# New float64 conversion steps and new planner costs in an attention, experts and dense kernel

## The chip, the cores and the metric

The kernel runs on one core of one Trainium2 chip. The metric is the device time of one execution in microseconds (us). A core has five engines with a queue each, served in order: TensorE (PE, matmuls; PEld is its weight loads), VectorE (DVE), ScalarE (ACT), GpSimd (POOL) and SyncE (SP, which here only issues transfers). Queues of transfers hang on SP, ACT and POOL.

## The reference, cut to what matters

```python
# x (8, 8, 512, 64), state (8, 8, 32, 64)
xread = softmax(x @ state.T / 8) @ state           # per batch and head
sread = softmax(state @ x.T / 8) @ x
x = concat(xread, sread) -> (4352 tokens, 512)
# experts: 8 of them, each token goes to the one with the greatest logit
idx = argmax(normalise(x) @ normalise(expert_emb).T / tau)
out[idx == e] = gate * relu(x @ w1[e]) @ w2[e]     # w1 (8, 512, 1024), w2 (8, 1024, 512)
# dense network; w_in (512, 2048) and w_out (2048, 512) are float64
h = x @ w_in
return (h * clip(h + 3, 0, 6) / 6 @ w_out).astype(float32)
```

The two dense weights arrive as float64, so the kernel gets their bits as pairs of 32-bit words.

## The kernel before, in words

**Stages.** Attention goes batch by batch (8 batches) and writes every token's row to a buffer in DRAM. Routing gives each token a place in one of up to 41 slots of 128 tokens of one expert. Five leading slots belong to the expert with the most tokens and share its weights (QUAD and FIFTH); then come pairs of slots and single slots, each unit with weights of its own. Their results, sorted, go to DRAM, and the dense network takes them in 17 blocks of 256 tokens. All large products are done in three matmuls of float32r parts (high x high, high x low, low x high), so weights and activations are split into a high part (a cast) and a low part (the difference).

**Expert weights.** A load brings 512 KB into one of two raw buffers (`load_w`, lines 1231 and 1234, issued by SP). Each half is cast (line 1245, ACT or DVE) and its low part taken (line 1248, DVE or POOL). Matmuls of the first product are line 1409 (pairs and QUAD) and 1450 (singles), of the second line 1512.

**Dense network.** For a block, `Y` (lines 1575 and 1579) loads 256 rows; `F1` (line 1618) does 12 matmuls of 256 columns for each of 16 pieces m, then Relu (ACT, 1622), a product (DVE, 1625), a cast (ACT, 1629) and a low part (DVE, 1632); `F2` (line 1653) does 6 matmuls of 512 columns. F1 and F2 of piece m need the converted pieces ("i", m) and ("o", m).

**Conversion of the dense weights** (class `Conv`, function `convert`): 32 pieces of 128x512 float64. Eight are converted beside attention, six beside the leading slots, in two raw buffers of their own (`acr`). The other 18 follow when the leading slots are done (`opened`); their raw data lie in the second buffers of the tiles `yh` and `yw`, of which a block needs one pair, so there are two pieces at a time, and block 1 can't be loaded before the last piece has gone. A piece passes these steps:

- `load`: ACT issues the transfer (line 259 or 262).
- `cs` (DVE): line 271 shifts the top 16 bits of each number down to its exponent and writes it over the lowest 16 bits; line 272 masks the top mantissa bits into a new tile.
- `ct` (ACT): line 276 turns the exponents into those of bfloat16, in place; line 277 turns the mantissa bits into a float32 from 1 to 2.
- `cd` (DVE): line 281 puts the sign into the bfloat16, in place; line 282 adds the next 16 mantissa bits.
- `cp` (line 286, POOL, or DVE for late pieces): mantissa times signed power of two. Here the raw buffer is given back.
- `ch` (line 293, ACT): the high part. `cl` (line 296, POOL or DVE): the low part. Here the mantissa tile is given back.

So the exponents are 16-bit numbers 8 bytes apart, and mantissas lie side by side.

**Order.** The program runs a list scheduler (`Sched`, lines 39 to 126) when it is built. Every operation has a cost on one or more engines, a due time, operands and buffers of rings. The scheduler keeps a clock for each engine, takes the operation with the least start time plus a weight times its due time, lets it run on the cheaper engine where there are two, and emits it; that is the order of the queues. Due times come from a nominal order of TensorE's work (lines 1197 on) and of attention's batches (`OFF`), which the change leaves alone. For transfers of SP and ACT it also keeps a clock of the shared issue path:

```python
if e != "P":
    self.hw = b + 0.45 * (1 + o.cost[e] // 0.12)
```

Of the kernel before, what the change touches and what calls it, by code (L numbers as in the profile page):

```python
# [20 lines left out]
class Ring:  # L21
    """The buffers of a tag: the times from which those that nothing holds are free."""
# [5 lines left out]
class Hold:  # L28
    """A buffer of a ring, from the operation that takes it to the last of those that read it."""
# [9 lines left out]
class Sched:  # L39
    """Puts operations in the order of the engines' queues: by an estimate of the engines' times, an engine that  # L40
    is free takes the most urgent of the operations whose operands and buffers are there."""
# [9 lines left out]
    def op(self, fn, cost, prio, deps=(), take=(), give=(), dma=0.0, after=None):  # L51
        """After deps have ended, and behind after in the same queue."""
# [79 lines left out]
def kernel(  # L132
# [48 lines left out]
    # what is kept until the leading slots are done  # L181
# [40 lines left out]
    # ring buffers  # L222
# [12 lines left out]
    # the attention's end, the leading slots' end, and the end of the slots that may be left out  # L235
# [65 lines left out]
    def convert(n, prio, pool, ma, gate=None, start=0.0):  # L301
        """Takes over a piece: into the buffers of pool, from gate on."""
# [29 lines left out]
    # columns of the tokens: those of the last batches come last, BA before them  # L332
# [18 lines left out]
    # the state twice, for its transpose on both halves of the partitions  # L351
# [11 lines left out]
    # output row of every token slot of the internal order  # L363
# [3 lines left out]
    # as two numbers that bfloat16 holds  # L367
# [29 lines left out]
    # normalised expert embeddings over tau, transposed  # L397
# [15 lines left out]
    # state transposed, two heads block diagonal, its products with the embeddings, and its parts  # L413
# [49 lines left out]
    # ---- what is done with a batch  # L463
# [8 lines left out]
    # the first batches in larger pieces, with the heads outside  # L472
# [37 lines left out]
    # those of the reads of the tokens in parts, of the rows r0 to r1 of every partition  # L510
# [19 lines left out]
    # the scores with their signs turned, and their least ones: less the greatest scores  # L530
# [132 lines left out]
    def o_lg(b, r):  # L663
        """The logits of rows ahead of these."""
# [41 lines left out]
    # ---- the operations of the attention  # L706
# [44 lines left out]
    # the times of a batch's operations in the order of their urgency, and the engines of those that two can do  # L751
# [13 lines left out]
    def batch(b, t, last):  # L765
# [5 lines left out]
        def do(name, f, cost, *a, args=(), late=0.0, **k):  # L771
            """An operation of this batch; by the engine in BY if two can do it."""
# [33 lines left out]
        for v in range(2):  # L806
            e2.append(do("e2", o_e2, {"A": 0.664}, [mx[v]], [be2] if v == 0 else (), [hsc], args=(v,), late=v,
                         after=e2[-1] if e2 else None))
        r2 = do("r2", o_r2, {"D": 0.28}, e2)
        sd = do("sd", o_sd, {"P": 3.06}, g_ready[b], [bsd])  # L810
        for (r0, r1), scs in zip(chunks, scs_):
# [8 lines left out]
            nm = do("nm", o_nm, {"P": 0.1 + 0.00172 * n, "D": cd(n)}, [rc], args=rr)  # L820
# [6 lines left out]
        a2c = do("a2c", o_a2c, {"A": 0.904, "D": 1.131}, [a2], [ba2], [ha2])  # L827
# [4 lines left out]
        V["sxo", b] = do("sx", o_sx, {"D": 0.81}, [sr, r2], [sx_h[q]] if b % 4 == 0 else (), [hsr])  # L832
        late, w, a = 0, [], None
        lga_[b] = []
        for r in range(R):
# [5 lines left out]
            w.append(do(f"x{r}c", o_xrc, {"A": 0.491, "D": 0.615}, [a], (), [hp], args=(r,), late=r))  # L841
# [1027 lines left out]
```

## Time and profile before

| | us |
|---|---|
| median of 3 runs (least, greatest) | 1454.6 (1453.09, 1455.71) |
| span of the profiled execution | 1453.4 |
| PE busy in it | 1354.7 (93%), 8976 matmuls |
| DVE busy | 917.8 (63%) |
| ACT busy | 645.3 (44%) |
| POOL busy | 543.1 (37%) |

No time of the profiled execution as a whole is recorded beside its span; the median of the runs is 1.2 us above the span. The page cuts the span into 40 slices of 36.3 us; a digit is an engine's busy share in tenths:

```profile
PE   7896697877799999999999999999999999999997
DVE  6988888899976555645454544665666675433332
```

Busy time of an engine includes the time for which an instruction, once started, waits inside. A matmul counts as busy for as long as it takes, at whatever clock. Idle time of an engine that isn't the one that sets the pace costs nothing.

### The profile page before, as it was taken

What the parts mean: (1) busy time and instruction counts of PE and PEld (TensorE: products, weight loads), DVE (VectorE), ACT (ScalarE), POOL (GpSimd) and SP (SyncE); (2) the same over time, 40 slices, a digit from 0 to 9 for tenths busy, and PEclk for the clock granted to TensorE, in tenths of its full rate; (3) what the DMA queues carried; (4) which work ended last, traced back from release to release, by engine and by line L of the source; (5) the groups of instructions that cost most, each with busy time, mean ns of one, the idle gap of its engine ahead of it and who ended that gap; (6) DMA issues with size and microseconds to landing.
All of it is one profiled execution on the core that took longest, in us unless ns stands there. A gap on an engine that the chain in (4) does not pass through costs nothing. (4 is left out here: it accounts for less than half of the span.)

```text
span 1453.4 us, 25243 instructions
## 1 busy us (share of the span) xinstructions
PE 1354.7 (93%) x8976; PEld 1199.0 (82%) x8976; DVE 917.8 (63%) x2008; ACT 645.3 (44%) x1347; POOL 543.1 (37%) x558
## 2 busy tenths in 40 slices
PE   7896697877799999999999999999999999999997
PEld 6675686766688898989989898999998999899996
DVE  6988888899976555645454544665666675433332
ACT  4785435555643343434444343555544444333332
POOL 5554448566555232524142322244344322200000
PEclk8996689899899999999999999999999999999999
DMA  6643435555564333423243333555455544201000
GB/s 162 175 160 116 148 96 161 156 188 159 157 182 149 94 115 89 136 82 124 90 125 98 108 104 100 154 150 177 152 148 153 174 139 140 74 23 30 15 16 15
DMA packets 151765, 175.64 MB, mean 121 GB/s; under 512 B 43784, under 2 KB 116488, under 8 KB 150608
## 3 DMA queue, kind: packets, MB, share of 16 engines
q1 hardware_dynamic: 128544, 121.19, 28.2%
q0 software_dynamic: 12336, 35.99, 8.2%
q10 hardware_dynamic: 10752, 16.78, 3.6%
q8 instruction: 73, 1.20, 0.4%
q14 instruction: 60, 0.49, 0.1%
HBM read 146.09 MB, written 27.82 MB: 120 GB/s over the span
## 5 line engine op out<-in xcount | busy, mean ns | idle before, releaser
L1618 PE MATMUL u_ps<-yh,wih 128*128 128x256 f32 x1088 | 306.9, 282 | 6.0 <-DVE gl L1632 4.3
L1618 PE MATMUL u_ps<-yh,wil 128*128 128x256 f32 x1088 | 306.8, 282 | 3.1 <-DVE wil L296 3.1
L1618 PE MATMUL u_ps<-yw,wih 128*128 128x256 f32 x1088 | 307.0, 282 | 0.0
L1248 POOL TENSOR_TENSOR wl<-raw,wh 128x512 fp32r<-128x512 f32 x129 | 176.6, 1373 | 274.4 <-ACT wh L1245 127.3
L1625 DVE SCALAR_TENSOR_TENSOR u_ps<-r,u_ps 128x256 f32<-128x256 f32 x272 | 116.2, 427 | 255.0 <-ACT r L1622 240.5
L1622 ACT ACTIVATE r<-u_ps,three 128x256 f32<-128x256 f32 x272 | 129.1, 475 | 305.4 <-PE u_ps L1618 277.2
L1618 PEld LDWEIGHTS u_ps<-yh,wih 128*128 128x128 f32 x1088 | 207.3, 191 | 17.2 <-DVE gl L1632 4.3
L1653 PE MATMUL o<-woh,gh 128*128 128x512 f32 x544 | 217.0, 399 | 2.0 <-DVE yo L1667 1.2
L1653 PE MATMUL o<-wol,gh 128*128 128x512 f32 x544 | 216.4, 398 | 0.0
L1653 PE MATMUL o<-woh,gl 128*128 128x512 f32 x544 | 214.9, 395 | 0.0
L1618 PEld LDWEIGHTS u_ps<-yw,wih 128*128 128x128 f32 x1088 | 206.6, 190 | 8.5
L1618 PEld LDWEIGHTS u_ps<-yh,wil 128*128 128x128 f32 x1088 | 207.5, 191 | 3.3 <-DVE wil L296 3.3
L1512 PE MATMUL y_ps<-wh,hx 128*128 128x512 f32 x512 | 186.3, 403 | 1.3 <-DVE wh L1245 1.3
L1629 ACT CAST gh<-u_ps 128x256 fp32r<-128x256 f32 x272 | 101.2, 372 | 187.9 <-PE o L1653 140.4
L1248 DVE TENSOR_TENSOR wl<-raw,wh 128x512 fp32r<-128x512 f32 x223 | 160.5, 727 | 33.4 <-ACT wh L1245 29.6
L1632 DVE TENSOR_TENSOR gl<-u_ps,gh 128x256 fp32r<-128x256 f32 x272 | 114.4, 421 | 98.0 <-ACT gh L1629 94.3
L1276 POOL DMA_INDIRECT xq<-xd,qidx x128 | 136.1, 1063 | 54.0 <-issue 31.9
L1245 ACT CAST wh<-raw 128x512 fp32r<-128x512 f32 x197 | 120.9, 619 | 73.3 <-PE y_ps L1512 39.8
L1409 PE MATMUL h_ps<-xt,wh 128*128 128x256 f32 x704 | 140.9, 288 | 3.8 <-ACT wh L1245 3.8
L1672 POOL DMA_INDIRECT out_dram<-yo,ix x34 | 35.9, 1057 | 273.3 <-ACT gh L1629 160.0
L1653 PEld LDWEIGHTS o<-woh,gl 128*128 128x128 f32 x544 | 102.6, 189 | 25.2
L1409 PEld LDWEIGHTS h_ps<-xt,wh 128*128 128x128 f32 x704 | 117.6, 197 | 5.7 <-ACT wh L1245 4.2
(312 smaller groups left out, 2474.2 us busy)
## 6 DMA issues: line engine op xcount, KB each, us to landing
raw<-in_moe_w_dram SPq DMA_DIRECT2D x176, 512.0 KB
yl<-ysd SPq DMA_DIRECT2D x136, 64.0 KB
xd<-xr SPq DMA_DIRECT2D x8, 1056.0 KB
ysd<-yt POOLq DMA_DIRECT2D x32, 256.5 KB
xb<-in_x_dram SPq DMA_DIRECT2D x48, 128.0 KB
yw<-in_moe_w_out_dram ACTq DMA_DIRECT2D x9, 512.0 KB
cv_raw<-in_moe_w_in_dram ACTq DMA_DIRECT2D x8, 512.0 KB
yh<-in_moe_w_in_dram ACTq DMA_DIRECT2D x8, 512.0 KB
```

Source lines behind the costliest of these rows:

```text
L1245: copy[e](pc["hi"], box["t"][:, j, :])
L1248: eng[e].tensor_tensor(pc["lo"], box["t"][:, j, :], f32(pc["hi"]), op=ALU.subtract)
L1276: POOL.indirect_dma_start(q[:, j * QW:(j + 1) * QW], None, xd_q, index(qidx[:, j, s:s + 1]))
L1409: PE.matmul(out(f), pc[w][:, (2 * c + f) * 128:(2 * c + f + 1) * 128], u.xt[a][:, 2 * j + c, 256 * hf:256 * hf + 256], start=new and c == ...
L1512: PE.matmul(u.y[i], u.ht[t][:, a, lo + 128 * i:lo + 128 * i + 128], pc[w], start=c == 0 and k == 0, stop=c == KF - 1 and k == 2)
L1618: PE.matmul(p, w, y[:, k, :], start=k == 0 and j == 0, stop=k == KD - 1 and j == 2)
L1622: ACT.activation(q["r"], q["p"], AF.Relu, bias=pool["three"][:, 0:1])
L1625: DVE.scalar_tensor_tensor(q["p"], q["r"], 6.0, q["p"], op0=ALU.min, op1=ALU.mult)
L1629: ACT.copy(q["h"], q["p"])
L1632: DVE.tensor_tensor(q["l"], q["p"], f32(q["h"]), op=ALU.subtract)
L1653: PE.matmul(o["o"][a], g[:, a * 128:(a + 1) * 128], w, start=m == 0 and j == 0, stop=m == KFF - 1 and j == 2)
L1672: POOL.indirect_dma_start(out, bass.IndirectOffsetOnAxis(ap=o["ix"][:, a:a + 1], axis=0), box["t"], None)
```

## The change

The conversion is cut in other steps. The exponents get a tile of their own (where the mantissa was), side by side; the mantissa stays in the raw tile, in the upper word of each number. `cs` keeps only the exponent's step, the mask moves to `cd`, the mantissa's conversion to float becomes a step `cu` (ACT) behind `cd`, and the addition of the low bits a step `cm` (DVE) behind that. The raw buffer (`hr`) is now given back by `cl`, the small tile (`hc`) by `cp`.

Most costs of the scheduler are new and greater, but not those of attention's matmuls. The rest of the diff takes comments out.

```diff
         def cs(self, pool):
             self.ma = self.raw
             if self.wide:
                 h = self.raw.bitcast(U16).rearrange("p (f w) -> p f w", w=4)
-                self.ex, self.low, self.sign = h[:, :, 0], h[:, :, 1], h[:, :, 3]
-                self.ma = pool()
-                top = self.raw.rearrange("p (f w) -> p f w", w=2)[:, :, 1]
+                self.low, self.sign = h[:, :, 1], h[:, :, 3]
+                self.top = self.raw.rearrange("p (f w) -> p f w", w=2)[:, :, 1]
+                self.ma = self.top.bitcast(F32)
+                self.ex = pool().bitcast(U16)[:, 0:512]
                 DVE.tensor_scalar(self.ex, self.sign, 4, 0x7FF, op0=ALU.logical_shift_right, op1=ALU.bitwise_and)
-                DVE.tensor_scalar(self.ma.bitcast(I32), top, 0xFFFFF, None, op0=ALU.bitwise_and)
 
         def ct(self):
             if self.wide:
                 ACT.activation(self.ex, self.ex, AF.Relu, bias=ebias[:, 0:1], scale=2.0**7)
-                ACT.activation(self.ma, self.ma.bitcast(I32), AF.Copy, bias=1.0, scale=2.0**-20)
 
         def cd(self):
             if self.wide:
                 DVE.scalar_tensor_tensor(self.ex, self.sign, 0x8000, self.ex, op0=ALU.bitwise_and, op1=ALU.bitwise_or)
+                DVE.tensor_scalar(self.top, self.top, 0xFFFFF, None, op0=ALU.bitwise_and)
+
+        def cu(self):
+            if self.wide:
+                ACT.activation(self.ma, self.top, AF.Copy, bias=1.0, scale=2.0**-20)
+
+        def cm(self):
+            if self.wide:
                 DVE.scalar_tensor_tensor(self.ma, self.low, 2.0**-36, self.ma, op0=ALU.mult, op1=ALU.add)
...
-        a = last_conv[0] = op(lambda: c.load(pool), {"A": 0.06}, prio - 8, [gate], [hr], dma=1.46, after=last_conv[0])
+        a = last_conv[0] = op(lambda: c.load(pool), {"A": 0.36}, prio - 8, [gate], [hr], dma=1.46, after=last_conv[0])
         a.ready = start
-        b = op(lambda: c.cs(ma), {"D": 0.67}, prio, [a], [hc])
-        d = op(c.ct, {"A": 1.13}, prio, [b])
+        b = op(lambda: c.cs(ma), {"D": 0.6}, prio, [a], [hc])
+        d = op(c.ct, {"A": 0.62}, prio, [b])
         e = op(c.cd, {"D": 1.2}, prio, [d])
-        f = op(*((lambda: c.cp("P"), {"P": 1.225}) if early else (c.cp, {"D": 0.6, "P": 1.225})), prio, [e], (), [hr])
-        g = op(c.ch, {"A": 0.52}, prio, [f, home])
-        dense[conv_q[n]] = op(*((lambda: c.cl("P"), {"P": 1.225}) if early else (c.cl, {"D": 0.6, "P": 1.225})), prio, [g], (), [hc])
+        e = op(c.cu, {"A": 0.68}, prio, [e])
+        e = op(c.cm, {"D": 0.72}, prio, [e])
+        f = op(*((lambda: c.cp("P"), {"P": 1.3}) if early else (c.cp, {"D": 0.68, "P": 1.3})), prio, [e], (), [hc])
+        g = op(c.ch, {"A": 0.62}, prio, [f, home])
+        dense[conv_q[n]] = op(*((lambda: c.cl("P"), {"P": 1.3}) if early else (c.cl, {"D": 0.68, "P": 1.3})), prio, [g], (), [hr])
...
-            return 0.052 + 0.000832 * n
+            return 0.16 + 0.00083 * n
...
-            return 0.064 + 0.00104 * n
+            return 0.15 + 0.00104 * n
...
-        ld = last_raw[0] = op(load, {"S": 0.06}, prio[0] - 4, deps, [hr], dma=1.46, after=last_raw[0])
+        ld = last_raw[0] = op(load, {"S": 0.45}, prio[0] - 4, deps, [hr], dma=1.46, after=last_raw[0])
...
-            a = op(hi, {"A": 0.52, "D": 0.335}, prio[j], [ld], [pc["hold"]], [hr])
-            pc["op"] = op(lo, {"D": 0.6, "P": 1.225}, prio[j], [a], (), [hr])
+            a = op(hi, {"A": 0.62, "D": 0.42}, prio[j], [ld], [pc["hold"]], [hr])
+            pc["op"] = op(lo, {"D": 0.68, "P": 1.3}, prio[j], [a], (), [hr])
...
-            ld = last_y[0] = op(load, {"S": 0.3}, prio - 5.3354, deps, [hr] if a else [hr, o["ix"]], dma=0.8, after=last_y[0])
+            ld = last_y[0] = op(load, {"S": 1.9}, prio - 5.3354, deps, [hr] if a else [hr, o["ix"]], dma=0.8, after=last_y[0])
...
-        a = last_f[1] = op(mm, {"T": 1.306}, prio, [*o["ready"], dense.get(("i", m)), *deps], [hu],
+        a = last_f[1] = op(mm, {"T": 1.41}, prio, [*o["ready"], dense.get(("i", m)), *deps], [hu],
...
-        f = last_f[2] = op(mm, {"T": 1.29}, prio, [ready, dense.get(("o", m)), *deps],
+        f = last_f[2] = op(mm, {"T": 1.41}, prio, [ready, dense.get(("o", m)), *deps],
```

## Rows read from the trace of the kernel before

**Rows 1.** By stretch: busy us (instructions) of PE, PEld, DVE, ACT, POOL; PEclk, DMA, GB/s.

```profile
40.00:140.00 100.00, 82.59 (x882) 68.02 (x879) 92.51 (x175) 70.45 (x111) 53.42 (x88) 0.89 0.49 151
150.00:265.00 115.00, 94.62 (x532) 80.72 (x532) 94.49 (x234) 53.27 (x108) 69.28 (x62) 0.81 0.48 141
265.00:410.00 145.00, 112.76 (x604) 95.91 (x604) 140.07 (x225) 83.43 (x151) 90.33 (x69) 0.89 0.51 157
460.00:1280.00 820.00, 818.06 (x5265) 738.57 (x5265) 465.00 (x1068) 348.34 (x782) 275.09 (x258) 1.00 0.42 124
```

**Rows 2.** Chain that ended last, dense tail: start us, duration us, what.

```profile
1287.84 1.43 PE u_ps L1618 x12
...
1290.66 1.44 PE u_ps L1618 x12
```

**Rows 3.** Table by stretch, PE lines 1512, 1653, 1409, 1618 alone, in turn.

```profile
265.00:410.00 145.00, 35.52 (x119) 24.84 (x120) 0.89 0.51 157
...
265.00:410.00 145.00, 25.18 (x90) 17.59 (x90) 0.89 0.51 157
...
265.00:410.00 145.00, 30.39 (x203) 27.66 (x202) 0.89 0.51 157
...
265.00:410.00 145.00, 29.25 (x192) 27.63 (x192) 0.89 0.51 157
```

**Rows 4.** Table by stretch, DVE lines 271, 272, 281, 282 alone, in turn.

```profile
265.00:410.00 145.00, 15.72 (x18) 0.89 0.51 157
...
265.00:410.00 145.00, 13.09 (x18) 0.89 0.51 157
...
265.00:410.00 145.00, 26.13 (x18) 0.89 0.51 157
...
265.00:410.00 145.00, 21.72 (x18) 0.89 0.51 157
```

**Rows 5.** Conversion lines: ns min/median/max, first and last start us, shapes.

```profile
L271 DVE TENSOR_SCALAR yw<-yw x9: 725/746/1839, 265.1 to 389.7; 128x512 uint16<-128x512 uint16 x9
...
L272 DVE TENSOR_SCALAR cv_m<-yw x9: 428/464/3205, 265.6 to 390.2; 128x512 int32<-128x512 int32 x9
...
L276 ACT ACTIVATE yw<-yw,ebias x9: 1424/1465/1495, 268.1 to 390.5; 128x512 uint16<-128x512 uint16 x9
...
L277 ACT ACTIVATE cv_m<-cv_m x32: 629/687/706, 48.8 to 401.5; 128x512 f32<-128x512 int32 x32
...
L281 DVE SCALAR_TENSOR_TENSOR yw<-yw x9: 1302/1322/1374, 272.5 to 392.0; 128x512 uint16<-128x512 uint16 x9
...
L282 DVE SCALAR_TENSOR_TENSOR cv_m<-yw,cv_m x9: 706/729/1717, 273.7 to 393.1; 128x512 f32<-128x512 uint16 x9
```

**Rows 6.** Groups by line and shape, DVE, 110 to 220 us: busy us, mean ns | idle before.

```profile
L964 DVE TENSOR_TENSOR bts<-place,iqj 128x1152 bf16<-128x1152 bf16 x2 | 1.7, 851 | 0.0
```

**Rows 7.** Timeline, ACT and DVE, a turn of the buffer yw: start us, duration us.

```profile
295.69 0.33 ACTq L262 DMA_DIRECT2D yw<-in_moe_w_out_dram  x1
...
297.43 0.68 DVE L296 TENSOR_TENSOR wol<-cv_m,woh 128x512 fp32r<-128x512 f32 x1
...
300.34 1.84 DVE L271 TENSOR_SCALAR yw<-yw 128x512 uint16<-128x512 uint16 x1
...
311.97 0.33 ACTq L262 DMA_DIRECT2D yw<-in_moe_w_out_dram  x1
```

**Rows 8.** Timeline, DVE and POOL, 289 to 295 us.

```profile
289.85 0.73 DVE L282 SCALAR_TENSOR_TENSOR cv_m<-yh,cv_m 128x512 f32<-128x512 uint16 x1
...
290.71 2.53 POOL L1248 TENSOR_TENSOR wl<-raw,wh 128x512 fp32r<-128x512 f32 x2
290.81 4.24 DVE L1248 TENSOR_TENSOR wl<-raw,wh 128x512 fp32r<-128x512 f32 x1
293.20 1.29 POOL L286 TENSOR_TENSOR cv_m<-cv_m,yw 128x512 f32<-128x512 f32 x1
```

**Rows 9.** Timeline, SP, 250 to 270 us.

```profile
253.32 5.22 SPq L1579 DMA_DIRECT2D yl<-ysd  x8
```

More of the change, by code (lines that the diff above doesn't have):

```diff
@@ L806, in batch @@
         for v in range(2):
-            e2.append(do("e2", o_e2, {"A": 0.664}, [mx[v]], [be2] if v == 0 else (), [hsc], args=(v,), late=v,
+            e2.append(do("e2", o_e2, {"A": 0.89}, [mx[v]], [be2] if v == 0 else (), [hsc], args=(v,), late=v,
                          after=e2[-1] if e2 else None))
-        r2 = do("r2", o_r2, {"D": 0.28}, e2)
-        sd = do("sd", o_sd, {"P": 3.06}, g_ready[b], [bsd])
+        r2 = do("r2", o_r2, {"D": 0.44}, e2)
+        sd = do("sd", o_sd, {"P": 3.6}, g_ready[b], [bsd])
         for (r0, r1), scs in zip(chunks, scs_):
@@ L831, in batch @@
             sx_h[q] = hold("sx")
-        V["sxo", b] = do("sx", o_sx, {"D": 0.81}, [sr, r2], [sx_h[q]] if b % 4 == 0 else (), [hsr])
+        V["sxo", b] = do("sx", o_sx, {"D": 1.15}, [sr, r2], [sx_h[q]] if b % 4 == 0 else (), [hsr])
         late, w, a = 0, [], None
@@ L840, in batch @@
                 lga_[b].append(do("lg", o_lg, {"D": 0.3}, [a], (), [hp], args=(r,), late=r))
-            w.append(do(f"x{r}c", o_xrc, {"A": 0.491, "D": 0.615}, [a], (), [hp], args=(r,), late=r))
+            w.append(do(f"x{r}c", o_xrc, {"A": 0.6, "D": 0.69}, [a], (), [hp], args=(r,), late=r))
         j = col(b)
@@ L1364, in X @@
             hm, hp = hold("gps"), hold("gp")
-            a = op(perm, {"A": 0.56, "D": 0.5}, prio, [og], [u.hx, hp] if i == 0 else [hp], [hg])
+            a = op(perm, {"A": 0.81, "D": 0.56}, prio, [og], [u.hx, hp] if i == 0 else [hp], [hg])
             b = u.tr = op(tr, {"T": 0.434}, prio, [a], [hm], [hp], after=u.tr)
-            c = op(xh, {"A": 0.478}, prio, [b])
-            u.x.append(op(xl, {"D": 0.602}, prio, [c], (), [hm]))
+            c = op(xh, {"A": 0.59}, prio, [b])
+            u.x.append(op(xl, {"D": 0.68}, prio, [c], (), [hm]))
         else:
@@ L1371, in X @@
             a = last_q[0] = op(parts, {"P": 4.16}, prio - 4, ready, [hq], dma=0.75, after=last_q[0])
-            b = u.tr = op(blocks, {"D": 0.66}, prio, [a], [u.hx] if i == 0 else (), after=u.tr)
-            c = op(bh, {"A": 0.53, "D": 0.4}, prio, [b])
-            u.x.append(op(bl, {"D": 0.67}, prio, [c], (), [hq]))
-        o1 = op(g1, {"D": 0.28}, late, [og], [hgate], [hg])
-        o2 = op(g2, {"A": 0.613}, late, [a if lead else og, o1], (), [hg])
-        o3 = op(g3, {"P": 0.464}, late, [o2])
-        o4 = op(g4, {"D": 0.34}, late, [o3, o1])
-        o5 = op(g5, {"A": 0.286}, late, [o4])
-        o["gate"] = op(g6, {"D": 0.27}, late, [o5], (), [hgate])
+            b = u.tr = op(blocks, {"D": 0.81}, prio, [a], [u.hx] if i == 0 else (), after=u.tr)
+            c = op(bh, {"A": 0.82, "D": 0.56}, prio, [b])
+            u.x.append(op(bl, {"D": 0.83}, prio, [c], (), [hq]))
+        o1 = op(g1, {"D": 0.32}, late, [og], [hgate], [hg])
+        o2 = op(g2, {"A": 0.82}, late, [a if lead else og, o1], (), [hg])
+        o3 = op(g3, {"P": 0.58}, late, [o2])
+        o4 = op(g4, {"D": 0.52}, late, [o3, o1])
+        o5 = op(g5, {"A": 0.49}, late, [o4])
+        o["gate"] = op(g6, {"D": 0.31}, late, [o5], (), [hgate])
         if lead:
@@ L1415, in L1w @@
         last = (q, j) == (3, 1) and hf == u.n // 2 - 1
-        a = u.l1 = op(mm, {"T": 1.28}, prio, [*xd_, pc["op"]], u.h[q] if new else (),
+        a = u.l1 = op(mm, {"T": 1.4}, prio, [*xd_, pc["op"]], u.h[q] if new else (),
                       [pc["hold"]] + ([u.hx] if last else []), after=u.l1)
@@ L1432, in lo @@
                 DVE.scalar_tensor_tensor(t[:, 1], u.hp[q][f], 0.0, f32(t[:, 0]), op0=ALU.max, op1=ALU.subtract)
-            b = op(hi, {"A": 0.478}, prio, [a], [hh])
-            u.r[n] = op(lo, {"D": 0.602}, prio, [b], (), [u.h[q][f]])
+            b = op(hi, {"A": 0.6}, prio, [a], [hh])
+            u.r[n] = op(lo, {"D": 0.68}, prio, [b], (), [u.h[q][f]])
     def L1(u, k, prio):
@@ L1456, in relu @@
             ACT.activation(u.hs[v], u.hp[v], AF.Relu)
-        a = u.l1 = op(mm, {"T": 0.645}, prio, [*u.x, pc["op"]], [u.h[v]] if k % 4 == 0 else (), [pc["hold"]], after=u.l1)
+        a = u.l1 = op(mm, {"T": 0.7}, prio, [*u.x, pc["op"]], [u.h[v]] if k % 4 == 0 else (), [pc["hold"]], after=u.l1)
         if k % 4 == 3:
-            u.r[v] = op(relu, {"A": 0.478}, prio, [a], (), [u.h[v]])
+            u.r[v] = op(relu, {"A": 0.6}, prio, [a], (), [u.h[v]])
             if u.lead:
@@ L1481, in HT @@
         a = u.l1 = op(tr, {"T": 0.434}, prio, [u.r[v]], [hm, hh], [u.hx] if v else (), after=u.l1)
-        b = op(hi, {"A": 0.478}, prio, [a])
-        u.r["t", v] = op(lo, {"D": 0.602}, prio, [b], (), [hm])
+        b = op(hi, {"A": 0.59}, prio, [a])
+        u.r["t", v] = op(lo, {"D": 0.69}, prio, [b], (), [hm])
     last_out = [None]
@@ L1543, in yd @@
                 POOL.dma_start(ysd[bass.ds(cv, 128), :], o["yt"])
-        b = op(ya, {"A": 0.571}, prio, [a, o["gate"]], [hy], [yh])
-        c = op(yb, {"D": 0.07}, prio, [b])
-        o["out"] = op(yd, {"S": 0.06} if u.lead else {"P": 1.04}, prio, [b, c, None if u.lead else cs_op] + ([] if u.lead else [slots[k]["out"] for k in range(NL)]),
+        b = op(ya, {"A": 0.69}, prio, [a, o["gate"]], [hy], [yh])
+        c = op(yb, {"D": 0.15}, prio, [b])
+        o["out"] = op(yd, {"S": 0.36} if u.lead else {"P": 1.1}, prio, [b, c, None if u.lead else cs_op] + ([] if u.lead else [slots[k]["out"] for k in range(NL)]),
                       (), [hy], dma=0.73, after=None if u.lead else last_out[0])
@@ L1597, in lo @@
                 DVE.tensor_tensor(view(1), src(), f32(view(0)), op=ALU.subtract)
-            ld = last_y[0] = op(load, {"S": 0.3}, prio - 5.3354, deps, [hr] if a else [hr, o["ix"]], dma=0.8, after=last_y[0])
-            b = o["tr"] = op(tr, {"D": 0.602}, prio - 1.8572, [ld], [o["yT"]] if a == 0 else (), after=o.get("tr"))
-            c = op(hi, {"A": 0.478, "D": 0.335}, prio - 1.8572, [b])
-            o["ready"].append(op(lo, {"D": 0.602}, prio - 1.8572, [c], (), [hr]))
+            ld = last_y[0] = op(load, {"S": 1.9}, prio - 5.3354, deps, [hr] if a else [hr, o["ix"]], dma=0.8, after=last_y[0])
+            b = o["tr"] = op(tr, {"D": 0.71}, prio - 1.8572, [ld], [o["yT"]] if a == 0 else (), after=o.get("tr"))
+            c = op(hi, {"A": 0.62, "D": 0.42}, prio - 1.8572, [b])
+            o["ready"].append(op(lo, {"D": 0.69}, prio - 1.8572, [c], (), [hr]))
     last_f = {1: None, 2: None}
```

16 lines of the change are left out of this document (8 added, 8 removed).

## The prediction

> **What bounds the kernel now.** I read the page first: TensorE is at 9 in nearly every slice of the second two thirds and lower in the first third, where VectorE stands at 8 and 9. So the question is which stretches have TensorE time to give back. The table by stretch [rows 1] splits the span where the kernel's stages change. From 460 to 1280 us TensorE is busy 818.06 of 820 us at a granted clock of 1.00, the level of 2.4 GHz: there no order of the work and no shorter VectorE instruction can save anything. From 265 to 410 us VectorE is busy 140.07 of 145 us while ScalarE (83.43) and GpSimd (90.33) have slack.
>
> TensorE's busy figure hides what that stretch loses, because a waiting or slowly clocked matmul counts as busy. So I count matmuls. In the tail the chain of waits repeats a pair of dense steps, 12 matmuls of 256 columns and 6 of 512, every 2.82 us (1290.66 less 1287.84) [rows 2]. With 512 columns taken as twice 256, that is 24 units: 0.1175 us per 256 columns, 0.235 us per 512. From 265 to 410 us TensorE does 119 and 90 matmuls of 512 and 203 and 192 of 256 columns [rows 3]: 209 x 0.235 + 395 x 0.1175 = 95.5 us of work in 145 us, so 49.5 us are lost there (in waits, and in a granted clock of 0.89 on average). All 18 late pieces of the dense weights are converted in this stretch, and lines 271, 272, 281 and 282, the four steps that split and rejoin a float64, hold VectorE for 15.72 + 13.09 + 26.13 + 21.72 = 76.7 us of its 140 [rows 4]. That is the largest single user of the engine that bounds the stage.
>
> The earlier stages are like it in kind. In attention, 40 to 140 us, VectorE is busy 92.51 of 100 us, from 150 to 265 us 94.49 of 115 [rows 1]. Eight pieces are converted beside attention and six beside the leading slots.
>
> **The change, conversion first.** Medians of one 128x512 step now: exponent out of the top half 0.746, mantissa mask 0.464, Relu on the exponents (ScalarE) 1.465, mantissa to float 0.687 (ScalarE), sign into the exponent 1.322, low bits into the mantissa 0.729 [rows 5]. VectorE per piece: 0.746 + 0.464 + 1.322 + 0.729 = 3.26 us. Measured it is 76.7 / 18 = 4.26 us, so about 1.0 us of each piece is waiting inside the instruction.
>
> What is slow is narrow writing at a step: line 281 and line 282 are the same operation on the same count and both read 16-bit numbers 8 bytes apart, but 281 also writes 16-bit numbers 8 bytes apart and takes 1.322, where 282 writes 32-bit numbers and takes 0.729 [rows 5]. Contiguous 16-bit output is not slow in this trace: 1152 bfloat16 in a row are written in 0.851 us [rows 6].
>
> The Trainium skill speaks against this (Advanced Engine Details and Errata, SBUF Cachelines): a line is 16 bytes, and two hits on a line are enough for full performance. By that rule a step of 8 bytes, two hits a line, is free, so laying the exponents side by side saves nothing and the time is that of rival 2. The trace bears it out for reading (line 282) and not for writing (line 281).
>
> New prices, with both ends:
> - Sign into exponent, now contiguous output: between 0.729 (line 282) and 1.322 (unchanged). I take 0.73, the row nearest in everything but the output. Saved 0.59.
> - Exponent out, now contiguous output, one operand: between 0.464 (line 272) and 0.746. I take the middle, 0.60. Saved 0.15.
> - Mask and mantissa sum, now in place in the raw tile at 8-byte steps of 32-bit words: the mask read such words already. 0.464 to 0.75 and 0.73 to 0.90; I take them unchanged.
> - Relu on ScalarE, now contiguous: between 0.687 (line 277) and 1.465. I take 0.70, saving 0.76 of ScalarE per piece. ScalarE is at 83 of 145 us, so this counts as nothing by itself; if ScalarE were the cover that is gone, it would be up to 18 x 0.76 = 14 us.
>
> So VectorE saves 0.74 us a piece (0 to 0.88). From 265 to 410 us: 18 x 0.74 = 13.3 us. VectorE being at 97% there, I count each freed microsecond as one of the stage: 13. Its ends are 0, if the freed time turns into waiting, and 20: half of TensorE's work there is experts, 119 x 0.235 + 203 x 0.1175 = 52 us, for which some 35 us of VectorE were left, so each freed microsecond can admit 1.5 us of matmuls. Attention: 8 x 0.74 = 5.9, VectorE at 93%: 5 (0 to 7). Leading slots: 6 x 0.74 = 4.4, VectorE at 82%: 3 (0 to 5). Together 21 us.
>
> **What it adds.** The mantissa now stays in the raw tile, so that buffer is given back by the low part (cl) instead of by the product (cp), and the next load, issued by ScalarE, waits for it. Two new handoffs (cd to cu, cu to cm) lengthen the chain. Behind a waiting load on ScalarE's queue stand the casts of expert weights and the Relu and cast of the dense step, and TensorE waits for these. Now a buffer turns over in 311.97 - 295.69 = 16.3 us, and the load comes before the piece's low part, which ends at 298.11 [rows 7]: 2.4 us later per turn. Beside that 0.69 for cu has moved behind cd instead of beside ct, and 0.59 + 0.15 + 0.76 are saved. The chain alone, from the load's issue to the first step 4.65 us [rows 7], then 0.60, 0.70, 0.73, 0.46, 0.69, 0.73, a product at 1.29 [rows 8], a cast at ScalarE's 0.69 and a low part at 1.29 or 0.68, comes to 11.2 to 11.8 us. A turn of 16.3 leaves some 4.5 us for the handoffs, so I cost it at nothing; without that cover see the first rival.
>
> **The planner's costs.** They decide the order and, for some operations, the engine. The old plan gave the four VectorE steps 0.67 + 1.2 = 1.87 us a piece where 4.26 are used: 2.39 x 18 = 43 us of VectorE that it did not see from 265 to 410 us, so it kept sending splits there while GpSimd stood at 62%. The new one gives 0.60 + 1.2 + 0.72 = 2.52. I take 4 us for a better division, with ends -15 (another order can be worse in attention, one more wait of 2 us in each of eight batches) and +25 (half of the 49.5 lost). One new cost is off: line 118 counts a transfer's cost in steps of 0.12 as 0.45 us each of the shared issue path, so a weight load now blocks it for 1.8 us and a block's load for 7.2, where eight of the block's transfers were issued in 5.22 us [rows 9]. The plan will think weights late and put dense steps ahead. Behind 460 us that costs nothing, as TensorE is full either way; before, it is within the -15.
>
> **Sum.** 13 + 5 + 3 + 4 = 25 us. The profiled execution spans 1453.4 us; the median of the runs, 1454.6, is 1.2 above it, which I leave as it is: 1453.4 - 25 + 1.2 = 1429.6, so 1430 us.
>
> **Rivals.**
> 1. Slower: the conversion becomes bound by its handoffs. Place: 265 us on. In the trace a handoff to a busy engine costs up to 2.6 us: a mantissa sum ended at 290.58 and its product on GpSimd began at 293.20 [rows 8]. Three more such waits (cu, cm, the load behind cl) are 7.9 us a turn, less the 1.5 saved: 6.4 x 9 turns = 58 us, in which block 0 is the only dense work, as the second pair of its buffers holds the raw pieces. If TensorE fills 66% of that, as it does now (95.5 / 145), 20 us are lost, against 8 saved in the earlier stages: 1466. It decides from an average wait of 4.5 / 3 = 1.5 us per handoff. For it: ScalarE's queue is in order and each late load stops it. Against it: ScalarE and GpSimd have 40% slack.
> 2. No change: the price lies in the 16-bit type or the rule on lines holds, and nothing on VectorE gets shorter: 1454. Against it: the pair 281/282 and the contiguous bfloat16 row.
> 3. Half the gain: the freed time goes to waiting for GpSimd. A VectorE split that takes 0.68 alone took 4.24 us, from 290.81 to 295.05, ending just after GpSimd's two splits and a product (to 294.49) [rows 8]. In the 18 pieces such waits are 76.7 - 18 x 3.26 = 18 us now, and a plan that sends more splits to GpSimd makes more of them: half of 21 is left, 1444. The Trainium skill has this as a rule (SBUF — State Buffer, SBUF: two separate sides): a VectorE instruction with two SBUF inputs and a GpSimd one that reads SBUF exclude each other for a whole instruction; the 4.24 us agree.
> 4. Larger: the plan levels VectorE with GpSimd and ScalarE and half of the 49.5 us comes back beside the conversion's share: 25 further, 1405.
>
> **Chances.** Forecast 0.42 (own range 1415 to 1441), rival 1 0.20, rival 2 0.12, rival 3 0.13, rival 4 0.13. The range 1405 to 1465 leaves out half of rivals 1 and 4, some 0.17. A measurement here tells about 0.2%, 2.9 us, from no change. Faster by more: 0.42 + 0.13 + 0.12 + 0.03 of rival 2 = 0.70; within: 0.08; slower: 0.20 and 0.02 of rival 2 = 0.22.
>
> **What would show it.** Right: the sign step falls from 1.32 to about 0.73 and the Relu from 1.465 to about 0.70; from 265 us on more matmuls per microsecond (over 0.66 of full), with VectorE below 97%; conversions done by about 410; the stretch from 460 on merely shifted earlier. Wrong: the sign step stays above 1.1; or a buffer's turn above 19 us with the conversions ending past 430; or attention ending later than now (140 us).

## Result and the profile after

| | before | after |
|---|---|---|
| median of the runs shown together (least, greatest) | 1454.5 (1453.1, 1455.7) | 1475.8 (1474.7, 1479.1) |
| span of the profiled execution | 1453.4 | 1473.8 |
| DVE busy | 917.8 | 896.6 |
| ACT busy | 645.3 | 615.2 |
| POOL busy | 543.1 | 567.0 |

The change makes the kernel slower: ratio 1.0147, 95% interval 1.0133 to 1.0162, about 21 us. VectorE and ScalarE are busy for less time, and yet the end comes later.

The steps themselves fell as predicted. Conversion lines of the kernel after (ns least/median/greatest, first and last start):

```profile
L273 DVE TENSOR_SCALAR cv_m<-yw x9: 407/417/1385, 277.7 to 402.7; 128x512 uint16<-128x512 uint16 x9
...
L277 ACT ACTIVATE cv_m<-cv_m,ebias x32: 705/722/732, 47.3 to 411.0; 128x512 uint16<-128x512 uint16 x32
...
L281 DVE SCALAR_TENSOR_TENSOR cv_m<-yw,cv_m x9: 676/692/693, 279.0 to 403.9; 128x512 uint16<-128x512 uint16 x9
L282 DVE TENSOR_SCALAR yw<-yw x9: 427/428/431, 279.8 to 404.6; 128x512 int32<-128x512 int32 x9
...
L290 DVE SCALAR_TENSOR_TENSOR yw<-yw x9: 681/693/3372, 282.6 to 406.0; 128x512 f32<-128x512 uint16 x9
```

Beside [rows 5]: exponent out 0.746 to 0.417, Relu 1.465 to 0.722, sign 1.322 to 0.692; mask and sum in place in the raw tile are no dearer (0.464 to 0.428, 0.729 to 0.693). One piece takes 2.23 us of VectorE where it took 3.26, so 1.03 us are saved and not the 0.74 predicted.

The table by stretch, which answers to [rows 1]:

```profile
40.00:140.00 100.00, 80.74 (x890) 66.89 (x887) 86.46 (x184) 65.51 (x108) 53.05 (x88) 0.91 0.49 154
150.00:265.00 115.00, 89.33 (x499) 75.35 (x499) 81.64 (x225) 48.06 (x107) 68.52 (x65) 0.83 0.43 131
265.00:410.00 145.00, 109.22 (x601) 94.67 (x602) 122.57 (x220) 70.59 (x141) 84.11 (x69) 0.88 0.52 159
460.00:1280.00 820.00, 814.57 (x5186) 734.53 (x5186) 471.76 (x1067) 333.25 (x752) 305.86 (x283) 1.00 0.42 126
```

VectorE is busy 122.57 of 145 us from 265 us on, where it was busy 140.07. It no longer bounds the stage, and TensorE does no more for it. I counted every matmul of the two traces by its columns at the rate of [rows 2], as time of work at the level of 2.4 GHz. By 240 us the kernel after is ahead, 139.6 us of work against 134.3. From 240 to 300 us it does 24.6 and the kernel before 39.9. At 440 us it is 11.4 behind, at 1200 us 12.2, at 1280 us 18.4.

Where the first of these losses begins shows in the timeline of the kernel after. Pieces 10 and 11 have their mantissa sums done at 233.60 and 236.49; GpSimd has gathers ahead of their products:

```profile
232.92 0.68 DVE L290 SCALAR_TENSOR_TENSOR cv_raw<-cv_raw 128x512 f32<-128x512 uint16 x1
...
235.80 0.69 DVE L290 SCALAR_TENSOR_TENSOR cv_raw<-cv_raw 128x512 f32<-128x512 uint16 x1 [0.89 <-ACT yt L1542]
...
230.77 1.05 POOL L1286 DMA_INDIRECT xq<-xd,qidx  x1 [0.30 <-issue]
...
240.40 0.94 POOL L1286 DMA_INDIRECT xq<-xd,qidx  x1 [0.30 <-issue]
241.36 2.27 POOL L294 TENSOR_TENSOR cv_raw<-cv_raw,cv_m 128x512 f32<-128x512 f32 x2
243.57 2.54 POOL L304 TENSOR_TENSOR wol<-cv_raw,woh 128x512 fp32r<-128x512 f32 x2
...
249.90 0.33 ACTq L263 DMA_DIRECT2D cv_raw<-in_moe_w_out_dram  x1
...
271.07 0.37 ACTq L263 DMA_DIRECT2D yw<-in_moe_w_out_dram  x1
```

The load of piece 12 may come only behind a low part (line 304, to 246.11), and it comes at 249.90. The last early piece ends at 273.8 (255.5 before), and the first late load is at 271.07 (259.17 before).

Dense work opens later still. Its first matmul, after and then before:

```profile
287.55 0.55 PE L1628 MATMUL u_ps<-yh,wih 128*128 128x256 f32 x1 [9.64 <-DVE yh L1604]
```

```profile
266.13 0.28 PE L1618 MATMUL u_ps<-yh,wih 128*128 128x256 f32 x1
```

TensorE stood 9.64 us for the second half of block 0's rows. On SyncE's queue that block's load stands behind a weight load that waits for its buffer, and comes in two halves 14 us apart (before, eight transfers in a row from 253.32 [rows 9]):

```profile
252.09 15.81 SPq L1244 DMA_DIRECT2D raw<-in_moe_w_dram  x2
...
268.65 1.78 SPq L1589 DMA_DIRECT2D yl<-ysd  x4
...
282.67 1.74 SPq L1589 DMA_DIRECT2D yl<-ysd  x4
```

From the first late load to the end of the last conversion the kernel after takes 147.4 us (271.07 to 418.46), the kernel before 147.9 (259.17 to 407.08). So the late stage begins 11.9 us late and is no shorter for its faster steps.

### The profile page after: what moved, and what is told of

It reads as the page before. It is cut to its first block, busy times and chain, and to the rows that moved or that the text cites. A ratio compares the mean times of both kernels' runs of the same rounds, so it can differ in the third digit from the quotient of the medians.

```text
span 1473.8 us, 25292 instructions
## 1 busy us (share of the span) xinstructions
PE 1355.3 (92%) x8976; PEld 1202.8 (82%) x8976; DVE 896.6 (61%) x2011; ACT 615.2 (42%) x1320; POOL 567.0 (38%) x582
## 5 line engine op out<-in xcount | busy, mean ns | idle before, releaser
L1258 POOL TENSOR_TENSOR wl<-raw,wh 128x512 fp32r<-128x512 f32 x159 | 216.4, 1366 | 346.6 <-ACT wh L1255 170.3
L1258 DVE TENSOR_TENSOR wl<-raw,wh 128x512 fp32r<-128x512 f32 x193 | 139.5, 734 | 28.7 <-ACT wh L1255 23.6
L1255 ACT CAST wh<-raw 128x512 fp32r<-128x512 f32 x183 | 111.3, 618 | 55.9 <-PE y_ps L1522 35.2
L1255 DVE CAST wh<-raw 128x512 fp32r<-128x512 f32 x169 | 88.3, 527 | 62.1 <-PE y_ps L1522 18.8
```

The lines of the kernel that those rows point to most:

```text
L1255: copy[e](pc["hi"], box["t"][:, j, :])
L1258: eng[e].tensor_tensor(pc["lo"], box["t"][:, j, :], f32(pc["hi"]), op=ALU.subtract)
```

## The experiments

Two theories stood at first. **H**: the raw buffer, now held through the low part, and the longer chain lose the time. **C**: the new costs of the planner make a worse order. All times are medians beside runs of the kernel before on the same chip, ratios with their 95% interval. Where two kernels ran beside different sets of runs of the kernel before, their difference is good to a microsecond or two. Line numbers in a row are those of its own kernel.

### One half of the change at a time

conv_only is before with the new conversion (the first part of the change's diff, its own steps at their new costs) and costs_only is after with the old one. loads_old and loads_new move only the transfers' costs, those of the results' writes with them:

```diff
# loads_new, to before (loads_old goes back from after)
-        a = last_conv[0] = op(lambda: c.load(pool), {"A": 0.06}, prio - 8, [gate], [hr], dma=1.46, after=last_conv[0])
+        a = last_conv[0] = op(lambda: c.load(pool), {"A": 0.36}, prio - 8, [gate], [hr], dma=1.46, after=last_conv[0])
...
-        ld = last_raw[0] = op(load, {"S": 0.06}, prio[0] - 4, deps, [hr], dma=1.46, after=last_raw[0])
+        ld = last_raw[0] = op(load, {"S": 0.45}, prio[0] - 4, deps, [hr], dma=1.46, after=last_raw[0])
...
-            ld = last_y[0] = op(load, {"S": 0.3}, prio - 5.3354, deps, [hr] if a else [hr, o["ix"]], dma=0.8, after=last_y[0])
+            ld = last_y[0] = op(load, {"S": 1.9}, prio - 5.3354, deps, [hr] if a else [hr, o["ix"]], dma=0.8, after=last_y[0])
```

> The kernel before with the new conversion alone; the planner's costs are those of before, only the three split steps and the two steps that are new in its list have the costs of the change. Theory H (the raw buffer, now held through the low part, and the two further handoffs delay the 14 early pieces and the start of the dense steps): the loss is in the conversion, so this one is slow too, 1468 to 1476 us, with the second load of a pair of early buffers some 20 us later than in the kernel before (249.9 against 228.1). Theory C (the new costs give a worse order, the conversion itself is the gain that was forecast): 1430 to 1445 us. Both at a half each: 1455 to 1465.

> The changed kernel with the conversion of before, its three split steps at their old costs; every other new cost stays. Theory H: near the kernel before, 1450 to 1460 us, early loads at 228 to 232. Theory C: 1470 to 1490 us (the loss of the change, 21 us, and no gain of the conversion against it).

> The changed kernel, with only the costs of transfers (weight loads, block loads, conversion loads, the results' writes) put back to 0.06, 0.3, 0.06 and 0.06/1.04 in the planner. Theory L (within C: the issue path that the plan believes busy for 1.8 us a weight load and 7.2 a block's load is what orders the early stage badly): 1440 to 1455 us, the block's second half loaded within 4 us of the first (14 in the changed kernel). Theory H, or C by the engines' costs: within 4 us of the changed kernel, 1472 to 1480.

> The kernel before with only the costs of transfers raised to those of the change (weight loads 0.45, block loads 1.9, conversion loads 0.36, results 0.36/1.1). Theory L: 1465 to 1478 us. Theory H, or C by the engines' costs: 1452 to 1458.

| | us | ratio to before |
|---|---|---|
| conv_only | 1466.8 | 1.0092 [1.0064, 1.0119] |
| costs_only | 1484.8 | 1.0224 [1.0192, 1.0256] |
| loads_old | 1481.3 | 1.0201 [1.0169, 1.0233] |
| loads_new | 1481.5 | 1.0195 [1.0164, 1.0227] |

Each half alone is slower than before, and the halves don't add up: 14 and 32 us, together 21. Transfers' costs cost 29 us on before, and taking them out of after costs another 5 to 8 (by medians and by ratios). Neither theory stands alone, and every one of these kernels has another order. How dense work opens doesn't settle it: in loads_old its first matmul is at 277.54, 10 us sooner than in after, and the kernel is slower all the same.

### The order held

So theory **O**: before has a lucky order, and any change of a cost loses it. early_held gives the exponents of the 14 early pieces a small tile of their own, with nothing else changed; the queues are the same, instruction by instruction. replay has the change's whole conversion in the order of before. jit_conv and jit_w move one cost by a hair.

```diff
# early_held (early pieces)
-                self.ex, self.low, self.sign = h[:, :, 0], h[:, :, 1], h[:, :, 3]
...
+                self.ex = h[:, :, 0] if ex is None else ex.bitcast(U16)[:, 0:512]
# replay: the planner's choice
-                        key = (b + (c if len(o.cost) > 1 else 0.0) + self.wp * o.prio, o.prio)
...
+                    if best is None or o.pos < best[0]:      # o.pos: its place in the order of before
# jit_conv, jit_w
-        d = op(c.ct, {"A": 1.13}, prio, [b])
+        d = op(c.ct, {"A": 1.15}, prio, [b])
...
-            a = op(hi, {"A": 0.52, "D": 0.335}, prio[j], [ld], [pc["hold"]], [hr])
+            a = op(hi, {"A": 0.53, "D": 0.34}, prio[j], [ld], [pc["hold"]], [hr])
```

> The kernel before, every queue in exactly its order, with the exponents of the 14 early pieces side by side in a small tile of their own (the mantissa keeps its tile, the raw buffer is given back where it was); the 18 late pieces are converted as before. Theory O (the kernel before has an order that happens to be good, each change of a cost or of the graph replaces it by another that is 14 to 30 us worse, and the conversion itself is a gain): 1447 to 1453 us, the 8 us of the prediction's attention and leading terms or a part of them. Theory H (the conversion costs time where it stands): 1453 us or more.

> The whole new conversion of the change, raw buffer held through the low part, with the queues in the order of the kernel before: the order is written into the kernel as a list, the two steps new to the list come right behind the sign step, and an instruction is put off only while its buffer is still held. Theory O: 1430 to 1445 us, the forecast of the prediction. Theory H: 1462 to 1476 us, like the new conversion with a plan of its own (1466.8).

> The kernel before with a single cost of its planner moved by 0.02 us (the ScalarE steps of a conversion, 1.13 to 1.15); no instruction is another, the order is. Theory O: 1460 to 1480 us, a loss of the size of the change's for nothing. Theory H and the theory that the change's costs are bad in themselves: 1450 to 1457.

> The kernel before with the planner's cost of a weight's first part moved by 0.01 and 0.005 us (0.52 to 0.53 on ScalarE, 0.335 to 0.34 on VectorE). Theory O: 1460 to 1480 us. Otherwise 1450 to 1457.

| | us | ratio to before |
|---|---|---|
| early_held | 1449.2 | 0.9973 [0.9960, 0.9986] |
| replay | 1474.1 | 1.0146 [1.0130, 1.0163] |
| jit_conv | 1454.5 | 1.0005 [0.9990, 1.0019] |
| jit_w | 1459.8 | 1.0048 [1.0031, 1.0065] |

Theory O falls: in these two tries a hair's change costs 0 to 7 us, not 20. Theory H gains: the new conversion is no faster in the good order than in its own (1474.1 against 1466.8), while the exponents' new place by itself is a gain.

### The conversion taken apart

all_held keeps the order and the chain of before, with the exponents of 29 pieces side by side; their late tile lies where the low part of the last piece of the first weight will stand. raw_held is all_held with the product written into the raw buffer, so that this is held through the low part. serial is all_held with mask and mantissa conversion behind the sign step. raw_soon gives the raw buffer back a step sooner, with a plan of its own. Where the expectations of the other three speak of the run beside them, or of the first, all_held is meant.

```diff
# all_held, to before
-                self.ex, self.low, self.sign = h[:, :, 0], h[:, :, 1], h[:, :, 3]
-                self.ma = pool()
+                self.low, self.sign = h[:, :, 1], h[:, :, 3]
+                self.ma, ex = pool()
+                self.ex = h[:, :, 0] if ex is None else ex.bitcast(U16)[:, 0:512]
...
+        cx[:] = [pool["wib"].tile([128, 256], F32, tag=n, name="cv_x") for n in ("wla", "wlb")]
# serial, to all_held
         def cd(self):
...
-                DVE.scalar_tensor_tensor(self.ma, self.low, 2.0**-36, self.ma, op0=ALU.mult, op1=ALU.add)
+                DVE.tensor_scalar(self.ma.bitcast(I32), self.top, 0xFFFFF, None, op0=ALU.bitwise_and)
+
+        def cu(self):
+            if self.wide:
+                ACT.activation(self.ma, self.ma.bitcast(I32), AF.Copy, bias=1.0, scale=2.0**-20)
+
+        def cm(self):
+            if self.wide:
+                DVE.scalar_tensor_tensor(self.ma, self.low, 2.0**-36, self.ma, op0=ALU.mult, op1=ALU.add)
# raw_held, to all_held (and hc, hr change places)
-                eng[e].tensor_tensor(self.ma, self.ma, self.ex.bitcast(BF16), op=ALU.mult)
+                p = self.raw[:, 0:512].bitcast(F32)
+                eng[e].tensor_tensor(p, self.ma, self.ex.bitcast(BF16), op=ALU.mult)
+                self.ma = p
# raw_soon, to all_held
-        e = op(c.cd, {"D": 1.2}, prio, [d])
+        e = op(c.cd, {"D": 1.2}, prio, [d], (), [hr])
...
```

> The kernel before with every queue in exactly its order and the exponents of 29 of the 32 pieces side by side in a tile of their own; the mantissa keeps its tile, mask and conversion to float stay ahead of the sign step, and the raw buffer is given back at the product, as before. The late pieces' exponents lie where the low part of the last piece of the first weight will stand (the last three pieces keep the old form). Theory R (the narrow writes are the gain that was forecast, and what the change pays is the raw buffer held through the low part): 1436 to 1445 us, by the prediction's 8 us of the early stages, of which the early pieces alone gave 4, and 15/18 of its 13. Theory G (the loss of the changed kernel in the late stage comes from the exponents' new place or the faster steps themselves): 1449 or more, no better than the early pieces alone.

> The same kernel as the run beside it (exponents of 29 pieces in their own tile, old chain), but the product is written into the raw buffer, so that this is given back by the low part and the next load waits for it; the queues keep their order but for these loads. Theory R: the turn of a late raw buffer goes from about 16 to about 18 us, nine turns are 18 us, and the time is 1455 to 1470. Theory S (the serial chain with its two handoffs is what costs): within 4 us of the run beside it.

> The same kernel as the first of this call, raw buffer given back at the product, but the mantissa's mask and its conversion to float come behind the sign step, one after the other, as in the change. Theory S: 1455 to 1470 us. Theory R: 1438 to 1450 us, at most a third of the loss, as the product comes 1 to 2 us later in a turn of 16.

> The same kernel as the first of this call, but the raw buffer is given back at the mantissa sum, one step sooner than in the kernel before, as neither exponents nor mantissa are in it any more; the planner puts the loads earlier and so makes an order of its own. Theory R: loads come 1 to 6 us sooner in a turn, the late conversions end by 395 us (407 before), and the time is 1425 to 1440 less or plus 6 for another order. Theory S or G: 1445 to 1460.

| | us | ratio to before | first late load | last conversion ends |
|---|---|---|---|---|
| before | 1454.1 | 1 | 259.2 | 407.1 |
| all_held | 1438.0 | 0.9894 [0.9874, 0.9914] | 250.2 | 388.9 |
| raw_held | 1457.6 | 1.0025 [1.0011, 1.0039] | 253.2 | 412.9 |
| serial | 1456.6 | 1.0019 [1.0006, 1.0032] | 261.4 | 408.4 |
| replay, both | 1474.1 | 1.0146 [1.0130, 1.0163] | 259.2 | 428.8 |
| raw_soon | 1448.5 | 0.9963 [0.9947, 0.9978] | 253.7 | 401.0 |
| after | 1475.8 | 1.0147 [1.0133, 1.0162] | 271.1 | 418.5 |

all_held beats both kernels, by 16 and by some 37 us. raw_held differs from it only in which buffer is held through the low part and is 19.6 us slower; serial is 18.5 slower, and both together (replay, with 32 pieces) 36.1. raw_soon came out 10 us above all_held and above what its expectation gave for theory R; it has an order of its own, and no run parts the two. The price of raw_held is a turn of the buffer. Timelines of all_held and then of raw_held, loads of yw on ScalarE's queue and the low part before them:

```profile
294.69 0.33 ACTq L262 DMA_DIRECT2D yw<-in_moe_w_out_dram  x1
...
299.56 1.72 DVE L306 TENSOR_TENSOR wol<-cv_m,woh 128x512 fp32r<-128x512 f32 x1
...
308.54 0.33 ACTq L262 DMA_DIRECT2D yw<-in_moe_w_out_dram  x1
```

```profile
295.06 0.33 ACTq L383 DMA_DIRECT2D yw<-in_moe_w_out_dram  x1
...
309.76 1.72 DVE L429 TENSOR_TENSOR wol<-yw,woh 128x512 fp32r<-128x512 f32 x1
...
311.51 0.34 ACTq L383 DMA_DIRECT2D yw<-in_moe_w_out_dram  x1
```

In raw_held the load starts 0.03 us after the low part has ended (309.76 + 1.72 = 311.48). In all_held it is out 5 us ahead of it. This turn is 13.85 there and 16.45 here; over all eight turns of yw it is 14.4 and 17.2 in the mean. From the first late load to the end of the conversions all_held takes 138.7 us and raw_held 159.7. What VectorE waited for at the exponent's step of the late pieces in raw_held (us, times) is the loads' landing:

```profile
  DMA yw<-in_moe_w_out_dram: 19.8, 7
  DMA yh<-in_moe_w_in_dram: 3.4, 4
```

In all_held it is 0.5 us, and in after, whose plan puts other work there, 5.0. So the 19.6 us, too, are the price in the order held, and not what after pays. TensorE's stretch, all_held and raw_held:

```profile
265.00:410.00 145.00, 117.81 (x676) 101.76 (x675) 132.47 (x251) 75.41 (x155) 86.31 (x74) 0.93 0.57 173
```

```profile
265.00:410.00 145.00, 104.35 (x559) 88.84 (x558) 112.76 (x216) 69.48 (x143) 76.16 (x63) 0.86 0.45 143
```

Under the serial chain VectorE idles ahead of the mantissa sum, which now waits for ScalarE. What it sat idle for at that line, in replay (serial has 23.4 us in 29 waits) and then in after:

```profile
  ACT cv_raw L406: 13.1, 14
  ACT yw L406: 6.6, 9
  ACT yh L406: 6.5, 9
```

```profile
  ACT yw L286: 2.0, 2
  ACT cv_raw L286: 1.1, 2
```

In the order held, the sum stands right behind the mask, and VectorE loses 26.2 us over 32 pieces. A plan of its own puts other work between them (3.1 us), so this price is not what after pays either. conv_only, planned anew, is 7 us faster than replay, and still 28.8 us slower than all_held.

### What is left: the planner's costs, and a load still sooner

held_tr and held_eng plan all_held's conversion with the change's costs of transfers and of engines; held_tr1 is held_tr without the count in line 118. soon_held and soon_late keep all_held's order and put only the loads earlier on ScalarE's queue, behind the mantissa sum of the piece two before: all of them, or only those of the late pieces.

```diff
# held_tr1, to held_tr
-                    self.hw = b + 0.45 * (1 + o.cost[e] // 0.12)
+                    self.hw = b + 0.45
# soon_late, to all_held (soon_held: n > 1)
+        if n > 15:
+            sc.behind = sum_at[n - 2].pos + 0.5
         a = last_conv[0] = op(lambda: c.load(pool), {"A": 0.06}, prio - 8, [gate], [hr], dma=1.46, after=last_conv[0])
...
-        e = op(c.cd, {"D": 1.2}, prio, [d])
+        e = sum_at[n] = op(c.cd, {"D": 1.2}, prio, [d], (), [hr])
...
```

> The kernel with exponents of 29 pieces in their own tile and the order of before (1438.0 us), in which only the conversions' loads are put earlier: each comes on ScalarE's queue as soon as the mantissa sum of the piece two before it is issued, since neither exponents nor mantissa are in the raw buffer any more; every other instruction keeps its place. If the raw buffer's turn still bounds the late pieces (13.9 us a turn): 1425 to 1434 us. If VectorE bounds them now (132.5 of 145 us busy): within 3 us of 1438.

> The same conversion, planned by the costs of before, but with the change's costs of transfers (weight loads 0.45, block loads 1.9, conversion loads 0.36, results 0.36/1.1). Theory T (the transfers' costs are what the planner's part loses): 1460 to 1470 us, with the last weights loaded late and TensorE waiting near 1230 to 1270. Theory E (the engines' costs): 1436 to 1446.

> The same with the change's costs of transfers, but each transfer takes 0.45 us of the shared issue path, whatever its cost (line 118 without the count). If the count in line 118 is what makes the transfers' costs bad: 1436 to 1448 us. If it is the costs on the queue itself, or the mere fact of another order: 1455 to 1470.

> The same conversion, planned by the change's costs of the engines (TensorE, ScalarE, VectorE, GpSimd) and by the transfers' costs of before. Theory E: 1455 to 1470 us. Theory T: 1436 to 1448, or a gain of up to 4 as the prediction had it.

> The order of before and the exponents of 29 pieces in their own tile (1438.0 us), with the earlier place of the load only for the 16 late pieces from the third on; attention and the leading slots have every instruction where it was. If what the kernel with all loads earlier lost (16 us) was lost in attention, where loads came some 9 us earlier into ScalarE's queue: 1430 to 1438 us. If a load that waits on ScalarE's queue for a VectorE step costs in the late stage too: 1440 to 1452.

| | us | ratio to before | beside all_held |
|---|---|---|---|
| held_tr | 1465.3 | 1.0081 [1.0056, 1.0106] | +27 |
| held_tr1 | 1457.2 | 1.0022 [1.0007, 1.0036] | +19 |
| held_eng | 1445.3 | 0.9939 [0.9919, 0.9958] | +7 |
| soon_held | 1454.2 | 1.0007 [0.9994, 1.0019] | +16 |
| soon_late | 1442.0 | 0.9925 [0.9901, 0.9948] | +4 |

The transfers' costs are the bad ones, the count of line 118 is 8 of their 27 us, and the engines' costs lose about what a hair's change can lose. Where the count shows is the last weights of the regular slots, loaded so late that TensorE has nothing left when the program branches on the number of slots used. TensorE's waits from 1180 to 1290 us (us, times, longest) in after, held_tr and held_tr1:

```profile
PE u_ps L1628 <- PEq L1837: 3.3, 1, 3.3
```

```profile
PE u_ps L1631 <- PEq L1842: 3.7, 1, 3.7
```

```profile
PE u_ps L1631 <- PEq L1842: 1.1, 1, 1.1
```

Before it was 0.9 us. loads_new and costs_only, with the new costs of transfers, wait 3.3 and 3.6 us there, loads_old, with the old ones, 1.2. In after the wait and the slow matmuls behind it (last section) make some 5 us, most of the step from 12.2 to 18.4 us behind between 1200 and 1280 us; this is an estimate from 3.27 us of waiting, 1.16 in the first 12 matmuls and 0.4 in the next three.

A load that comes sooner is no gain. On ScalarE's queue in soon_held:

```profile
51.82 0.37 ACTq L380 DMA_DIRECT2D cv_raw<-in_moe_w_in_dram  x1
52.29 1.01 ACT L737 COPY a<-a_ps 128x1024 f32<-128x1024 f32 x1 [3.00 <-DVE cv_m L404]
```

ScalarE stood 3.00 us for a mantissa sum on VectorE before it could issue the load, and attention's copy stood behind it. 12 of the 16 us are lost by the early loads (soon_held against soon_late), 4 by the late ones, whose conversions end at 397.7 instead of 388.9.

## Why the prediction was wrong

- **The conversion's steps: right, and the gain is real.** In the order and with the buffers of before, all_held gives 16 us (1438.0 against 1454.1) with 29 of 32 pieces; the prediction's 13 + 5 + 3 is 21. The late stage opens 9 us earlier (5 + 3 were put down for the early stages) and the late stage is 9.2 us shorter (147.9 to 138.7), where 15/18 of 13 is 11. The Trainium skill's rule on 16-byte lines (Advanced Engine Details and Errata, SBUF Cachelines), by which a step of 8 bytes is free, doesn't agree for 16-bit output: the exponent step, of which only the output moved, takes 0.746 us writing at that step and 0.417 side by side. The sign step went from 1.322 to 0.692, but there one of the two inputs moved too. The 35 us of VectorE behind the upper end of 20 stand in no row; that end was not reached.
- **"I cost it at nothing": the step that failed.** The raw buffer held through the low part and the two handoffs cost 36 us in the order held (replay against all_held), of which the held buffer alone makes 19.6. In a plan by the old costs they cost some 29 (conv_only against all_held, where the order differs too). The 4.5 us that I called cover did not take up the added step: with nothing else moved, the mean turn goes from 14.4 us (all_held) to 17.2 (raw_held). The turn of 16.3 that I read was one of eight, whose mean was 15.7. VectorE at 97% was not the only bound of the stage.
- **What of it shows in after.** The late stage takes 147.4 us, as before, where all_held takes 138.7; its mean turn is 15.8 us (15.7 before), so the faster steps are paid away there. The 11.9 us by which it begins late are no part of the 13 + 5 + 3. With the order held they are not there (replay's first late load is at 259.2), so they belong to after's order. conv_only begins 9.5 us late and costs_only, with the old conversion, 8.7: no run divides them between the held buffer and the costs.
- **The two handoffs.** serial shows 18.5 us with VectorE waiting at them. In after it idles 3.1 us at that line, and no run separates the handoffs from the held buffer in a plan of its own.
- **Rival 1: the place right, the number luck.** It named the held load and the handoffs, and its 1466 is near conv_only's 1466.8. But it had 8 us saved in the early stages and 20 lost in the late one; conv_only's late stage begins 9.5 us late and is 8.3 longer (156.2).
- **The planner's costs: +4 became a loss.** On the change's conversion they cost 8 to 9 us (conv_only to after, by ratios and by medians), on that of all_held 7 for the engines' and 27 for the transfers'. "Within the -15" was too little for the latter, and "behind 460 us that costs nothing" fell at the last weights. Of the 46 us from the forecast's 25 faster to 21 slower, some 34 are the conversion's (21 faster forecast, 13 slower in conv_only) and some 12 the costs'; this is an estimate by the ratios to before. The share stays open by more than that: the parts don't add up, as loads_old shows, and a hair's change moves up to 7 us.
- **What would show it.** The signs of failure that I named were too coarse: the eight turns of yw in after are 15.8 us in the mean (271.07 to 397.42) and only one, by 0.06, is above 19; the conversions end at 418.5, not past 430. The sign that told was VectorE falling to 85% without more matmuls (93.4 us of work from 265 to 410 us, 95.3 before).

## What to carry to other kernels

When a change frees the busiest engine but holds a buffer longer, work out the buffer's turn, from load to load, before the engine's share: in the order held, 2.8 us more in each turn of two buffers cost 19.6, and idle time inside the turn was not cover. To separate one edit's parts in a kernel that a list scheduler orders, replay the old order with each part alone. What that gives is the price in that order: a plan of its own can hide a part of it, and mixes in a change of order, here up to 7 us for a hair's change of a cost. And look at where a buffer is released: in one and the same order the exponents side by side made 1438 or, with the raw buffer held and the chain serial, 1474 us.

## What the runs showed of the hardware

16-bit numbers written 8 bytes apart are dear on VectorE (the exponent step, 0.746 us, side by side 0.417). ScalarE's 128x512 Relu on them takes 1.465 us at that step in and out and 0.722 side by side; no run parts its input from its output. 32-bit words written 8 bytes apart cost nothing that shows (mask 0.464 and 0.428, sum 0.729 and 0.693).

Behind a wait of 3.27 us TensorE was at its lower level for a while. In after, from 1270 to 1275 us the mean granted clock is 0.66, and the first 12 matmuls of 256 columns behind the wait take 2.59 us (1270.74 to 1273.33), where 12 take 1.43 at 1.00, the level of 2.4 GHz [rows 2]. Single ones start 0.21 us apart instead of 0.1175, near the level of 1.2:

```profile
1267.07 0.40 PE L1522 MATMUL y_ps<-wh,hx 128*128 128x512 f32 x1
1270.74 0.43 PE L1628 MATMUL u_ps<-yh,wih 128*128 128x256 f32 x1 [3.27 <-PEq L1837]
...
1273.33 0.63 PE L1663 MATMUL o<-woh,gh 128*128 128x512 f32 x1
```
